# Weights times v and state times q in four column quarters of TensorE in place of two halves

## The chip, the cores and the metric

The kernel runs on one core of a Trainium2 chip. The metric is device time in microseconds (us), the median of three runs. Inputs are laid out by the host before the launch and the host does no arithmetic.

## The reference, cut to what matters

An mLSTM recurrence over 768 tokens (4 sequences, 8 heads of 40) feeds a feed-forward block of width 2048.

```python
for t in range(S):
    m_new = np.maximum(f_gate[:, :, t] + m, i_gate[:, :, t])
    f_stab = np.exp(f_gate[:, :, t] + m - m_new)
    i_stab = np.exp(i_gate[:, :, t] - m_new)
    C = f_stab * C + i_stab * einsum('bhd,bhe->bhde', vt, kt)
    n = f_stab * n + i_stab * kt
    h_tilde = einsum('bhde,bhe->bhd', C, qt)
    denom = maximum(abs(einsum('bhd,bhd->bh', n, qt)), 1.0)
    y[:, :, t] = sigmoid(o_gate) * h_tilde / denom
...
h = x @ w_in                      # x: the 3072 tokens, 320 wide
g = h * erf(softplus(h))
return g @ w_out
```

## The kernel before

The recurrence is computed in six chunks of 128 tokens. A chunk `c` of one sequence `b` is an attention step, 24 in all (`attention(s)`, with `c, b = divmod(s, 4)`). Inside a chunk the tokens meet each other through a 128x128 matrix of decay times k·q for each head (`v.w[j]`, tile `dm`); the earlier chunks come in through a state (`st`) of 82 columns for each pair of heads, kept in SBUF, which is absent in the first chunk. The feed-forward block runs in 48 groups (`mlp(g)`), each over 512 hidden columns of 256 tokens: up-projection (line 817, PSUM tile `h`), a chain of Tanh and VectorE operations, down-projection (lines 886, 887, 889, PSUM tile `po`).

Every piece of work is put into one list with a start number from tables written out by hand. The list is sorted by that number and issued in this order, so that each engine works through a fixed queue. On TensorE (PE in the profile) attention steps lie in between pieces of the feed-forward block.

The pieces of an attention step that the prediction speaks of:

- `S0`, `S1` (line 578, tile `stk`): k·q, four products with all 128 columns of the array for each half of the heads.
- `pk` (line 633): the chunk's contribution to the state, eight products whose stationary operand has 40 columns; even heads use the left half of the array's columns (output partitions 0 to 39), odd heads the right half (64 to 103). The last chunk has no `pk`, since nobody needs its state.
- `ph` (lines 614 to 624): the numerator and the denominator for 128 tokens. For each of four pairs of heads `p` it multiplies state by q (line 619, 82 moving columns, only from the second chunk on) and, for each of the two heads, the weights by v (line 623, 41 moving columns). The stationary operands are q and the weights, and their columns are tokens. The tokens are cut in two halves of 64: the output of the first half goes to PSUM partitions 0 to 63, that of the second to 64 to 127, so that the two halves use different columns of the array.
- `den` and `yg` (lines 656 and 661) read the result on ScalarE and VectorE; `tr` (line 677) transposes the normalised output on TensorE.

A product of float32 operands, as in all of these, shows in the trace as two weight loads (PEld) and two MATMULs (PE), called passes here. The feed-forward products use float32r operands and show as one.

In chunks 1 to 4 `pk` stands right before `ph` on TensorE.

Of the kernel before, what the change touches and what calls it, by code (L numbers as in the profile page):

```python
# [351 lines left out]
def tile_mlstm_moe(  # L352
# [132 lines left out]
    def psum(n, m):  # L485
        t = ps_a.tile([128, 512], F32, name="pa")
        return t[:, 0:n * m].rearrange("p (n m) -> p n m", m=m)

    def attention(s):
# [11 lines left out]
        @at('load')  # L501
        def _():
            if stacked:
                v.q = att.tile([128, NPR, L], F32, name="q_t", bufs=QB)
                v.parts = att.tile([128, 4, NPR, L], F32R, name="parts")
                v.k = v.parts.bitcast(F32)[:, 3]
                nc.sync.dma_start(v.k[0:QR], qk[c, b, :, 1])
                nc.sync.dma_start(v.q[0:QR], qk[c, b, :, 0])
            else:
                t = att.tile([128, 2, NPR, L], F32R, name="stk", bufs=SB).bitcast(F32)  # L510
                nc.sync.dma_start(t[0:QR], qk[c, b])
                v.q, v.k = t[:, 0], t[:, 1]
# [100 lines left out]
        @at('ph')  # L613
        def _():
            v.ph = psum(H, V1)
            halves = [slice(64 * i, 64 * i + 64) for i in range(2)]
            for p in range(NPR):
                for ts in halves if c > 0 else ():
                    nc.tensor.matmul(v.ph[ts, 2 * p:2 * p + 2].rearrange("p h d -> p (h d)"),  # L619
                                     v.q[0:QR, p, ts], st[0:QR, p], start=True, stop=False)  # L620
                for j in range(2):
                    for ts in halves:
                        nc.tensor.matmul(v.ph[ts, 2 * p + j], v.w[j][:, p, ts], v.v1[:, 2 * p + j],  # L623
                                         start=(c == 0), stop=(c == 0 or j == 1))
# [357 lines left out]
```

## Time and profile before

| | |
|---|---|
| median of three runs | 512.31 us (512.07 to 512.38) |
| profiled execution | 514.03 us, of which the instructions span 512.0 us |
| TensorE (PE), share of the span | 485.7 us, 95% |
| weight loads (PEld) | 455.3 us, 89% |
| VectorE (DVE) | 439.0 us, 86% |
| ScalarE (ACT) | 449.9 us, 88% |
| GpSimd (POOL) | 82.0 us, 16% |
| granted clock of TensorE, mean | 0.993 |

Times in the views are microseconds from the start of the span unless marked ns. PE are the MATMULs and PEld the weight loads, which overlap them. MATMULs are pipelined, and their ends are modelled, so that the durations of neighbours overlap: the spacing of their starts is what TensorE takes for one.

### The profile page before, as it was taken

How to read it: one execution, taken by the hardware profiler on the slowest of the kernel's cores; microseconds unless marked ns; L12 is line 12 of the kernel's file. 1: busy time of each engine (PE TensorE's matmuls, PEld its weight loads, DVE VectorE, ACT ScalarE, POOL GpSimd, SP SyncE). 2: the span in 40 equal slices, each digit the busy share in tenths (PEclk: the TensorE clock that was granted, in tenths of full speed). 3: DMA queues.
4: the chain of work that ended last, by engine and by line, in shares of the span. 5: the costliest groups of instructions: out<-in, count | busy, mean ns of one | idle time of the engine just before them, and what ended most of it. 6: DMA issues, size and time to landing. Idle time of an engine off the chain costs nothing.

```text
span 512.0 us, 11875 instructions
## 1 busy us (share of the span) xinstructions
PE 485.7 (95%) x4630; PEld 455.3 (89%) x4630; DVE 439.0 (86%) x677; ACT 449.9 (88%) x714; POOL 82.0 (16%) x112
## 2 busy tenths in 40 slices
PE   2987999899999999999999999999999999999996
PEld 1654779799899999999999999999899999999996
DVE  4868899898999999989998989989988977877653
ACT  4757899998989999889989889989889989989993
POOL 3202002211121121121121121211111211110000
PEclk9889999999999999999999999999999999999999
DMA  7995643424424415505405515415415325300000
GB/s 249 276 260 128 195 118 102 130 86 126 142 59 138 151 40 159 167 14 163 156 13 174 157 22 168 144 40 164 125 40 166 124 69 154 105 15 14 2 26 27
DMA packets 28307, 58.93 MB, mean 115 GB/s; under 512 B 4156, under 2 KB 8764, under 8 KB 28252
## 3 DMA queue, kind: packets, MB, share of 16 engines
q1 hardware_dynamic: 28252, 58.18, 38.1%
q8 instruction: 37, 0.61, 0.5%
q14 instruction: 18, 0.15, 0.1%
HBM read 33.40 MB, written 3.93 MB: 73 GB/s over the span
## 4 chain that ended last, share of the span: by engine, by line
PE 67%; ACT 11%; DVE 10%; DMA 6%; issue 4%; SPq 1%; POOL 0%; DVEq 0%; ACTq 0%
PE h L817 26%; PE po L886 9%; PE po L889 8%; PE po L887 8%; DMA stk<-parts 4%; PE pa L578 3%; PE pa L623 3%; PE pa L619 2%; PE pa L724 2%; DVE bits L712 1%; PE pa L558 1%; PE pa L633 1%; ACT n L841 1%; DMA parts<-in_qk_dram 1%; PE pa L677 1%
## 5 line engine op out<-in xcount | busy, mean ns | idle before, releaser
L817 PE MATMUL h<-xh,wh 128*128 128x256 f32 x576 | 158.9, 285 | 0.8 <-ACT hb L827 0.8
L817 PE MATMUL h<-xl,wh 128*128 128x256 f32 x576 | 156.4, 281 | 0.2 <-DVE xl L690 0.2
L886 PE MATMUL po<-woh,gh 128*128 128x320 f32 x384 | 118.2, 318 | 1.1 <-ACT gh L867 1.1
L887 PE MATMUL po<-wol,gh 128*128 128x320 f32 x384 | 114.4, 308 | 0.0
L817 PEld LDWEIGHTS h<-xh,wh 128*128 128x128 f32 x576 | 108.6, 188 | 2.6 <-ACT hb L827 1.0
L817 PEld LDWEIGHTS h<-xl,wh 128*128 128x128 f32 x576 | 108.6, 188 | 0.7 <-DVE xl L690 0.5
L817 PE MATMUL h<-xh,wl 128*128 128x256 f32 x384 | 107.7, 280 | 0.0
L889 PE MATMUL po<-woh,gl 128*128 128x320 f32 x384 | 79.2, 326 | 0.0
L569 POOL TENSOR_SCALAR_AFFINE_SELECT dm<-dm 128x512 f32<-128x512 f32 x48 | 47.0, 982 | 171.6 <-ACT dm L565 164.0
L886 PEld LDWEIGHTS po<-woh,gh 128*128 128x128 f32 x384 | 72.2, 188 | 2.3 <-ACT gh L867 1.3
L817 PEld LDWEIGHTS h<-xh,wl 128*128 128x128 f32 x384 | 72.2, 188 | 0.0
L887 PEld LDWEIGHTS po<-wol,gh 128*128 128x128 f32 x384 | 72.2, 188 | 0.0
L872 DVE TENSOR_TENSOR gl<-hb,gh 128x1024 fp32r<-128x1024 f32 x48 | 58.7, 1223 | 13.4 <-ACT gh L867 13.0
L862 DVE SCALAR_TENSOR_TENSOR hb<-n,hb 128x1024 f32<-128x1024 f32 x48 | 58.6, 1221 | 10.3 <-ACT n L858 10.1
L854 DVE SCALAR_TENSOR_TENSOR n<-n,n 128x1024 f32<-128x1024 f32 x48 | 61.6, 1284 | 4.7
L867 ACT ACTIVATE gh<-hb 128x1024 fp32r<-128x1024 f32 x48 | 50.9, 1060 | 13.2 <-DVE hb L862 10.2
L850 DVE SCALAR_TENSOR_TENSOR n<-n,hb 128x1024 f32<-128x1024 f32 x48 | 59.6, 1242 | 3.3 <-ACT n L841 3.3
L889 PEld LDWEIGHTS po<-woh,gl 128*128 128x128 f32 x384 | 61.5, 189 | 1.0
L833 ACT ACTIVATE n<-h 128x512 f32<-128x512 f32 x96 | 57.3, 597 | 1.3 <-PE h L817 1.3
L858 ACT ACTIVATE n<-n 128x1024 f32<-128x1024 f32 x48 | 51.4, 1071 | 5.9 <-DVE n L854 5.8
L827 ACT ACTIVATE hb<-h 128x512 f32<-128x512 f32 x96 | 54.6, 604 | 1.6 <-DVE gl L872 0.7
L837 ACT ACTIVATE n<-n 128x1024 f32<-128x1024 f32 x48 | 51.1, 1064 | 1.0
(102 smaller groups left out, 821.1 us busy)
## 6 DMA issues: line engine op xcount, KB each, us to landing
stk<-parts SPq DMA_DIRECT2D x120, 160.0 KB
kvo<-in_kvo_dram SPq DMA_DIRECT2D x24, 484.0 KB
parts<-in_w_out_dram SPq DMA_DIRECT2D x5, 960.0 KB
parts<-in_qk_dram SPq DMA_DIRECT2D x20, 208.0 KB
q_t<-in_qk_dram SPq DMA_DIRECT2D x20, 208.0 KB
out_dram<-o_sb SPq DMA_DIRECT2D x24, 160.0 KB
stk<-in_qk_dram SPq DMA_DIRECT2D x4, 416.0 KB
hb<-in_w_in_dram SPq DMA_DIRECT2D x2, 512.0 KB
```

The costliest lines, as they stand in the source:

```text
L817: nc.tensor.matmul(v.h[n // 2][:, n % 2 * T:(n % 2 + 1) * T], w, m, start=(q == 0), stop=(q == len(ops) - 1))
L827: nc.scalar.activation(v.hb[:, hs], v.h[i], AF.Copy)
L833: nc.scalar.activation(v.a[:, hs], v.h[i], AF.Tanh, scale=PARAMS[0], bias=PARAMS[1])
L837: nc.scalar.activation(v.a, v.a, AF.Tanh, scale=PARAMS[2], bias=PARAMS[3])
L850: nc.vector.scalar_tensor_tensor(out=v.a, in0=v.a, scalar=PARAMS[8], in1=v.hb, op0=ALU.add, op1=ALU.mult)
L854: nc.vector.scalar_tensor_tensor(out=v.a, in0=v.a, scalar=PARAMS[9], in1=v.b, op0=ALU.mult, op1=ALU.add)
L858: nc.scalar.activation(v.a, v.a, AF.Tanh, scale=PARAMS[10], bias=PARAMS[11])
L862: nc.vector.scalar_tensor_tensor(out=v.hb, in0=v.a, scalar=1.0, in1=v.hb, op0=ALU.add, op1=ALU.mult)
L872: nc.vector.tensor_tensor(v.gl, v.hb, v.gh.bitcast(F32), op=ALU.subtract)
L886: nc.tensor.matmul(po[k, b], v.gh[:, ts], woh[:, w], start=(j == 0), stop=False)
L887: nc.tensor.matmul(po[k, b], v.gh[:, ts], wol[:, w], start=False, stop=False)
L889: nc.tensor.matmul(po[k, b], v.gl[:, ts], woh[:, w], start=False, stop=(j == NFF - 1))
```

## The change

The list `halves` that cuts the 128 tokens of a step gets four slices of 32 in place of two of 64. Both inner loops of `ph` run over it, so that each product becomes two, with half the stationary columns and the same moving columns. Slice i of the output goes to PSUM partitions 32i to 32i+31.

```diff
@@ -613,7 +613,7 @@
         @at('ph')
         def _():
             v.ph = psum(H, V1)
-            halves = [slice(64 * i, 64 * i + 64) for i in range(2)]
+            halves = [slice(32 * i, 32 * i + 32) for i in range(4)]
             for p in range(NPR):
                 for ts in halves if c > 0 else ():
                     nc.tensor.matmul(v.ph[ts, 2 * p:2 * p + 2].rearrange("p h d -> p (h d)"),
```

On TensorE's queue in a step of the second chunk, from the last up-projection before `ph` to its first pair of heads; the numbers behind a name are output partitions x moving columns, and x4 stands for four in a row. Before:

```order
L817 MATMUL h<-xl,wh 128x256
L578 MATMUL pa<-stk 128x128 x4
L633 MATMUL pa<-vg,kvo 40x41 x8
L619 MATMUL pa<-state_85,q_t 64x82 x2
L623 MATMUL pa<-kvo,dm 64x41 x4
```

And with the change:

```order
L817 MATMUL h<-xl,wh 128x256
L578 MATMUL pa<-stk 128x128 x4
L633 MATMUL pa<-vg,kvo 40x41 x8
L619 MATMUL pa<-state_85,q_t 32x82 x4
L623 MATMUL pa<-kvo,dm 32x41 x8
```

The pieces keep their places; for a pair of heads line 619 issues four products in place of two, line 623 eight in place of four.

On TensorE's queue in a step of the first chunk, as a difference (line 581 is k·q there, lines 724 and 725 unpack the weights of the feed-forward block):

```order
 L725 MATMUL pa<-woh,nident 128x320
 L581 MATMUL pa<-stk 128x128 x4
-L623 MATMUL pa<-kvo,dm 64x41 x16
+L623 MATMUL pa<-kvo,dm 32x41 x32
 L724 MATMUL pa<-bits,ident 128x320
 L725 MATMUL pa<-woh,nident 128x320
```

Here too nothing changes its place. The first chunk has no product with the state.

## Rows read from the trace of the kernel before

**Rows 1.** The page, parts 1 and 2: the span, busy time, granted clock in 40 slices.

```profile
span 512.0 us, 11875 instructions
PE 485.7 (95%) x4630; PEld 455.3 (89%) x4630; DVE 439.0 (86%) x677; ACT 449.9 (88%) x714; POOL 82.0 (16%) x112
PEclk9889999999999999999999999999999999999999
```

**Rows 2.** Busy time by stretch: PE, PEld, DVE, ACT, POOL, clock, DMA.

```profile
0.00:60.00 60.00, 44.02 (x290) 29.57 (x291) 43.84 (x96) 38.94 (x85) 11.19 (x30) 0.94 0.80 231
...
257.76:295.16 37.40, 37.40 (x396) 36.43 (x392) 34.92 (x56) 33.93 (x53) 6.25 (x8) 1.00 0.38 116
```

**Rows 3.** Chain that ended last, by line; then pieces of it: start, us, what.

```profile
by line: PE h L817 26.0%; PE po L886 9.0%; PE po L889 8.3%; PE po L887 8.1%; DMA stk<-parts 4.2%; issue 3.6%; PE pa L578 2.9%; PE pa L623 2.8%; PE pa L619 2.3%; PE pa L724 2.0%; DVE bits L712 1.5%; PE pa L558 1.3%; PE pa L633 1.3%; ACT n L8
...
220.53 0.16 PE pa L619 x4
220.70 0.21 PE pa L623 x8
...
354.87 6.84 DMA stk<-parts
```

**Rows 4.** PE in order of time around one `ph`: start, us, engine, line, operation, count.

```profile
220.03 0.51 PE L633 MATMUL pa<-vg,kvo 128*40 128x41 f32 x16
220.37 0.33 PE L619 MATMUL pa<-state,q_t 104*64 104x82 f32 x4
...
220.74 0.34 PE L619 MATMUL pa<-state,q_t 104*64 104x82 f32 x4
...
221.66 0.38 PE L623 MATMUL pa<-kvo,dm 128*64 128x41 f32 x8
221.97 0.41 PE L886 MATMUL po<-woh,gh 128*128 128x320 f32 x1
222.22 0.31 PE L887 MATMUL po<-wol,gh 128*128 128x320 f32 x1
222.37 0.31 PE L886 MATMUL po<-woh,gh 128*128 128x320 f32 x1
```

**Rows 5.** PEld in order of time in the same `ph`.

```profile
220.71 0.20 PEld L619 LDWEIGHTS pa<-state,q_t 104*64 104x64 f32 x4
220.84 0.33 PEld L623 LDWEIGHTS pa<-kvo,dm 128*64 128x64 f32 x8
221.08 0.20 PEld L619 LDWEIGHTS pa<-state,q_t 104*64 104x64 f32 x4
```

**Rows 6.** PE instructions of line 619 begun by the end of each stretch (in brackets).

```profile
220.36:220.37 0.01, 0.00 (x1) 1.00 0.00 0
220.36:220.38 0.01, 0.01 (x2) 1.00 0.00 0
```

**Rows 7.** Groups by line and shape: busy us, mean ns of one.

```profile
L623 PE MATMUL pa<-kvo,dm 128*64 128x41 f32 x768 | 34.8, 222 | 0.0
...
L677 PE MATMUL pa<-ident,kvo 128*128 128x128 f32 x72 | 12.1, 274 | 0.2 <-POOL kvo L671 0.2
L633 PE MATMUL pa<-vg,kvo 128*40 128x41 f32 x320 | 10.4, 209 | 0.0
...
L623 PEld LDWEIGHTS pa<-kvo,dm 128*64 128x64 f32 x768 | 30.7, 138 | 1.0 <-PE pa L724 0.5 <-issue 0.3
...
L633 PEld LDWEIGHTS pa<-vg,kvo 128*40 128x40 f32 x320 | 8.0, 120 | 2.9 <-PE pa L677 1.0 <-DVE bits L711 0.6 <-issue 0.4
```

**Rows 8.** PE in order of time where the last chunk's `ph` follows a transpose.

```profile
417.68 0.49 PE L677 MATMUL pa<-ident,kvo 128*128 128x128 f32 x3
418.10 0.36 PE L619 MATMUL pa<-state,q_t 104*64 104x82 f32 x4
```

**Rows 9.** PE in order of time, a `ph` of the first chunk.

```profile
35.73 1.13 PE L623 MATMUL pa<-kvo,dm 128*64 128x41 f32 x32
```

## The prediction

> **What bounds the kernel now.** I read the page first [rows 1]. PE is busy for 95% of the span, and its clock is granted in full (2.4 GHz, the higher of its two levels) from the second slice on. The profiled execution took 514.03 us, 1.7 us above the median of 512.31 us; I make the sum against it and carry the difference over.
>
> A busy share averages over stages, so I read the stretches next [rows 2]. In the first 60 us PE is busy for 44.0 us and waits for weights that are being unpacked. From 257.76 to 295.16 us, as in the other steady stretches, it is busy for all of 37.40 us, while DVE and ACT have 2.5 and 3.5 us to spare. There, time taken from PE is time taken from the kernel, as long as it is less than about 2 us in 37.
>
> The third view is the chain of waits [rows 3]. Line 619 has 2.3% of it and line 623 has 2.8%, of 512 us: 11.8 and 14.3 us. One `ph` puts four pieces of each on it, 0.16 and 0.21 us long, 0.64 and 0.84 us together. So some 17 or 18 executions of `ph` with the state lie on the chain. There are 20 of these (chunks 1 to 5), and the four of the first chunk, which have line 623 alone, find no place in the 14.3 us. I count 17, of which 13 come right behind `pk` and 4 are the last chunk's.
>
> **What one `ph` is made of.** In time order [rows 4] a group (one pair of heads: 4 passes of line 619, 8 of line 623) takes 220.74 - 220.37 = 0.37 us, four take 1.5 us. Passes start in twos: the first of line 619 by 220.37, the second by 220.38 us [rows 6], one in each half of the columns. I call such a pair a round; a group has 2 rounds of line 619 and 4 of line 623. The weight loads show where the time goes [rows 5]: from 220.71 to 220.84 for line 619, 0.13 us or 65 ns a round, and from 220.84 to 221.08 for line 623, 0.24 us or 60 ns a round. Line 623 streams 41 columns, half of line 619's 82, and still takes nearly as long. So streaming does not set its round; loading 64 columns of weights does. The neighbour `pk` confirms it: it streams the same 41 columns against 40 columns of weights, and its 8 rounds take 220.37 - 220.03 = 0.34 us, 42 ns each [rows 4]. One of its loads lasts 120 ns against 138 ns [rows 7], 0.75 ns for a column.
>
> **The change, part by part.** The passes of a `ph` go from 48 to 96 (from 32 to 64 in the first chunk), each with half the columns of weights. What counts is how many run side by side. If four quarters run abreast as two halves do now, a group still has 2 + 4 rounds, and only the length of a round changes.
>
> *Rounds of line 623.* Now 60 ns. With 32 columns of weights, at most the 42 ns of `pk` with 40; at least half of line 619's 65 ns, 33 ns, because 41 columns have to be streamed. I take 40 ns, close to the nearest row. Gain: 4 rounds x 20 ns x 4 groups = 0.32 us a `ph`, bounds 0.29 and 0.43.
>
> *Rounds of line 619.* They last 65 ns with loads that would allow 60, so streaming sets them and a shorter load gives nothing: 0.
>
> *Two more starts in each round.* Now the second start follows within 10 ns [rows 6]. The third and fourth could fall inside the round (0) or lengthen it by 10 ns each: 20 ns x 24 rounds = 0.48 us a `ph`. I take 0, since the second start today lies inside a round that its own load or stream fills, and keep 0.48 for the range.
>
> *The width changes between `pk` and `ph`.* Both use halves now: the last pass of `pk` begins at 220.03 + 0.51 - 0.20 = 220.34 us, and line 619 0.03 us later [rows 4]. Where the width changes, the trace shows a gap. The last transpose before the last chunk's `ph`, a full-width product, begins at 417.68 + 0.49 - 0.27 = 417.90 us, and line 619 at 418.10, 0.20 us later [rows 7, 8]. Behind a `ph`, the last pass begins at 221.66 + 0.38 - 0.22 = 221.82 us, the next product 0.15 us later, and that one takes 0.25 us where its neighbour takes 0.15 [rows 4, 7]. With the change `pk` stays in halves and `ph` goes to quarters. No row shows such a change: between 0 (as if it were none) and 0.23 us more (0.15 + 0.10 as at the exit, less a load of 32 columns). I take 0.15, the 0.20 of rows 8 less today's 0.03 and less 0.02 for the shorter load, since every change of width in the trace costs about that. It falls on the 13 executions behind `pk`.
>
> The Trainium skill (TensorEngine Tiling (Array Packing), section Tiling Modes) lists 64 and 32 columns as separate configurations and says that a change of configuration drains the engine while a change of tile does not. By that rule the 0.15 us is paid; without it the sum below would be -5.5 us. The trace agrees for full width against halves (0.20 and 0.03 us), and no run here shows halves against quarters yet.
>
> *The two other borders.* Entry from full width (the last chunk) gains the shorter load, 0.02 us; the exit to full width waits for the last pass as now: 0.
>
> *The first chunk.* Its four `ph` take 1.13 us each [rows 9] and would shorten by 16 rounds x 20 ns = 0.32 us, but none lies on the chain; nor do three of the later ones. I count 0 and keep 4 x 0.32 + 3 x 0.17 = 1.8 us as a bound on the gain.
>
> *Other engines.* DVE, ACT, POOL and the queues of DMA issues get the same work in the same order. Their cover in the steady stretches is 2.5 us in 37; a period holds two `ph`, which take some 0.35 to 0.7 us from it.
>
> **Sum.** 13 x (0.32 - 0.15) + 4 x (0.32 + 0.02) = 2.2 + 1.4 = 3.6 us gained; I say 3.5. The profiled execution would take 510.5 us, the median 508.8 us.
>
> **Rivals.**
>
> *Slower: PE is not fed twice as fast.* Doubling the passes pays only if they start at more than the rate of now. The fastest that the trace shows is `pk`, 16 passes in 0.34 us, 21 ns each; a `ph` in quarters wants 96 in about 1.2 us, 12 ns each. If 21 ns is the rate at which passes can be fed, a `ph` takes 96 x 21 ns = 2.0 us in place of 1.5: 0.5 us lost, 0.65 with the change of width; 13 x 0.65 + 4 x 0.5 = 10.5 us, a median of 523. It decides from 15.6 ns a pass (1.5 us / 96), without the width change. Against it: the two passes of a round of `pk` or line 619 start within 10 ns of each other and then nothing starts until the load or the stream is done, so 21 ns is a round divided by two and need not be a limit. Chance 0.13.
>
> The Trainium skill has a rule that speaks for this rival (TensorEngine Tiling (Array Packing), section Instruction Overhead): each matmul carries some 60 cycles of overhead, and a dimension that is already small should not be tiled for. By an estimate from that figure, 60 cycles at 2.4 GHz or 25 ns a pass in sequence, a `ph` would take 2.4 us and the kernel some 17 us more. Rows 6 do not bear it out as a cost in sequence, with two starts within 10 ns.
>
> *Slower: only two quarters run abreast.* Then a group has 4 rounds of 65 ns and 8 of 40 ns, 0.58 us against 0.37: 0.84 us a `ph`, with the width change 13 x 0.99 + 4 x 0.84 = 16 us, a median of 528. It would be so if PE looks ahead over few passes: a quarter's next work stands behind two passes of each of the three others, a half's behind two of one. No row shows how far it looks. Chance 0.07.
>
> *No change.* The starts lengthen the rounds by half of their bound (0.24 us a `ph`) and the width change costs its 0.23; or PE comes earlier and waits for something else, as it does at 354.87 us, where a DMA of 6.84 us lies on the chain [rows 3]. Then 512 us. Chance 0.14. That the edit does not do what it says has little room: the queue shows 32 partitions and twice the products in each place. I leave it in these 0.14.
>
> *The forecast* has the remaining 0.66.
>
> **Range and chances.** The forecast's own bounds: at best 13 x 0.43 + 4 x 0.45 + 1.8 = 9.2 us gained (503.1 us), with all borders free and all of the early gains kept; at worst, with the starts in sequence and the dear border, a loss of 13 x 0.4 + 4 x 0.15 = 5.8 us (518.1 us). Both ends need every unknown to fall on one side. The range from 504.5 to 513.0 us holds most of the forecast and the case of no change, and leaves out the two slower rivals, 0.2 together. A measurement of this kernel tells about 0.2% (1.0 us) from nothing. Faster by more: 0.66; within: 0.14; slower: 0.20.
>
> **What would show it.** In the profile after: weight loads of line 623 with 32 columns, near 114 ns (138 - 32 x 0.75); four passes of line 619 begun within some 20 ns; a group in about 0.29 us in place of 0.37; line 619 some 0.18 us behind the last pass of `pk`; stretches of 37.4 us shorter by 0.3 to 0.4 us, with PE still busy throughout. A group of 0.5 us or more, with passes spaced evenly at about 21 ns, makes the first rival right; a group near 0.58 us with starts in twos the second. A shorter `ph` with the same period would mean that PE was not the bound there, and my count of 17 on the chain was wrong.

## The result, and the profile after

The changed kernel takes 507.79 us in the median of ten runs (505.95 to 511.54), the kernel before 512.2 us (510.68 to 513.66) in runs on the same chip: a ratio of 0.9916 with a 95% interval of 0.9891 to 0.9941, 4.4 us less. The forecast was 508.8 us, in a range of 504.5 to 513.0.

The page of the changed kernel, parts 1 to 3 (span and busy time; the queue that brings instructions):

```profile
span 504.1 us, 14051 instructions
PE 478.0 (95%) x5718; PEld 447.5 (89%) x5718; DVE 438.5 (87%) x677; ACT 447.7 (89%) x714; POOL 82.2 (16%) x112
...
q8 instruction: 45, 0.74, 0.6%
```

There are 1088 more MATMULs and as many more weight loads than before [rows 1], and PE is busy for 7.7 us less. The spans of these two traces differ by 7.9 us, more than the change is worth: 1.6 us of it had passed before the first `ph` began (28.82 us here, 30.43 us before), a piece of the program that the change does not touch, and 1.7 us are waits of line 578 for the DMA of `stk` (4.1 us in the first trace of before, 2.4 here). The first of the two goes with the clock: ahead of the first `ph` TensorE was granted its lower level (1.2 GHz, 0.50 in the view) for 6.83 us before and for 3.41 us here. The same columns as in [rows 2], before and after:

```profile
21.75:28.58 6.83, 6.76 (x31) 4.54 (x32) 4.72 (x11) 4.13 (x10) 0.00 (x0) 0.50 1.04 264
```

```profile
23.90:27.31 3.41, 3.41 (x22) 2.01 (x18) 2.68 (x6) 2.23 (x5) 0.00 (x0) 0.50 1.04 333
```

The experiments take the rest apart.

Busy time by stretch, the period that answers to the second line of [rows 2] and the next one (PE, PEld, DVE, ACT, POOL, clock, DMA):

```profile
254.18:291.21 37.03, 37.03 (x487) 35.98 (x483) 34.95 (x56) 33.72 (x53) 6.18 (x8) 1.00 0.39 117
291.21:328.23 37.02, 37.02 (x487) 35.97 (x483) 35.05 (x54) 34.80 (x54) 7.80 (x9) 1.00 0.37 115
```

A period of two steps lasts 37.03 us in place of 37.40, and PE still has no gap in it; DVE and ACT do the work of before in less time.

One `ph` on PE in time order, as in [rows 4] (start, us, engine, line, operation, count), then three lines of its weight loads, as in [rows 5]:

```profile
253.80 0.45 PE L633 MATMUL pa<-vg,kvo 128*40 128x41 f32 x14
254.18 0.35 PE L619 MATMUL pa<-state,q_t 104*32 104x82 f32 x8
254.35 0.33 PE L623 MATMUL pa<-kvo,dm 128*32 128x41 f32 x16
254.50 0.33 PE L619 MATMUL pa<-state,q_t 104*32 104x82 f32 x8
254.64 0.33 PE L623 MATMUL pa<-kvo,dm 128*32 128x41 f32 x16
254.79 0.33 PE L619 MATMUL pa<-state,q_t 104*32 104x82 f32 x8
...
255.23 0.33 PE L623 MATMUL pa<-kvo,dm 128*32 128x41 f32 x16
255.50 0.42 PE L886 MATMUL po<-woh,gh 128*128 128x320 f32 x1
255.75 0.31 PE L887 MATMUL po<-wol,gh 128*128 128x320 f32 x1
```

```profile
254.47 0.17 PEld L619 LDWEIGHTS pa<-state,q_t 104*32 104x32 f32 x8
254.57 0.28 PEld L623 LDWEIGHTS pa<-kvo,dm 128*32 128x32 f32 x16
254.76 0.17 PEld L619 LDWEIGHTS pa<-state,q_t 104*32 104x32 f32 x8
```

A group lasts 254.79 - 254.50 = 0.29 us with 24 passes, where it lasted 0.37 us with 12. By the starts of the MATMULs line 619 holds 0.14 us of it (254.50 to 254.64, 72 ns a round) and line 623 0.15 us (38 ns a round). The prediction read its rounds from the starts of the weight loads, which divide a group otherwise, so each has to be compared with its like. By the loads, the two rounds of line 619 in a group went from 131 to 110 ns and the four of line 623 from 246 to 185 ns; by the MATMULs, from 172 to 144 and from 205 to 151 ns (medians over the later groups of all 20 `ph` with state). Both ways line 619 gives a part of what is saved.

The other ends of the `ph` moved too. The last pass of `pk` begins at 253.80 + 0.45 - 0.21 = 254.04 us and line 619 0.14 us later (0.130 us by the single starts), where it was 0.03. The last pass of line 623 begins at 255.23 + 0.33 - 0.20 = 255.36 us and the next full-width product 0.14 us later, where it was 0.15 (0.128 and 0.160 us by the single starts).

Groups by line and shape: mean duration in ns behind the busy time. A load of 32 columns lasts 110 ns (138 before; the prediction said 114).

```profile
L623 PEld LDWEIGHTS pa<-kvo,dm 128*32 128x32 f32 x1536 | 24.9, 110 | 1.0 <-PE pa L724 0.4 <-issue 0.3
```

MATMULs of line 619 begun by the end of each stretch, as in [rows 6]:

```profile
254.17:254.19 0.02, 0.01 (x2) 1.00 0.00 0
254.17:254.20 0.03, 0.02 (x3) 1.00 0.66 273
254.17:254.21 0.04, 0.03 (x4) 1.00 0.50 205
```

Four passes, one in each quarter, begin within 0.03 us, at most 10 ns apart; by the single starts of this row the next begins 95 ns behind the first. Quarters run abreast.

### The profile page after: what moved, and what is told of

It reads as the page before. It is cut to its first block, busy times and chain, and to the rows that moved or that the text cites. A ratio compares the mean times of both kernels' runs of the same rounds, so it can differ in the third digit from the quotient of the medians.

```text
span 504.1 us, 14051 instructions
## 1 busy us (share of the span) xinstructions
PE 478.0 (95%) x5718; PEld 447.5 (89%) x5718; DVE 438.5 (87%) x677; ACT 447.7 (89%) x714; POOL 82.2 (16%) x112
## 4 chain that ended last, share of the span: by engine, by line
PE 72%; ACT 12%; DVE 10%; issue 3%; DMA 2%; SPq 0%; POOL 0%; DVEq 0%; ACTq 0%
PE h L817 29%; PE po L886 10%; PE po L889 9%; PE po L887 9%; PE pa L578 3%; PE pa L619 3%; PE pa L623 2%; DVE bits L712 2%; PE pa L558 1%; PE pa L633 1%; DMA stk<-parts 1%; PE pa L677 1%; ACT gh L867 1%; DVE bits L711 1%; ACT bits L706 1%
```

## The experiments

### The change and the kernel before, a second trace of each

The change, with no edit:

> The changed kernel once more, for a second trace and a closer time. Theory (quarters run abreast, what is saved is saved at the executions of ph on the chain): each ph behind pk 0.19 us shorter (1.447 + 0.029 + 0.160 us became 1.185 + 0.130 + 0.129 in the first trace), each of the last chunk 0.32 us, together 13 x 0.19 + 4 x 0.32 = 3.8 us, or 5.6 us if all 24 count; ratio to before 0.989 to 0.993. Rival (the 7.9 us between the two spans is what the change is worth): ratio 0.985.

The kernel before, with no edit:

> The kernel before once more, for a second trace. Theory (the waits for DMA near 210 and 360 us, 0.9 and 1.2 us, and the slower first 30 us of its first trace are not the change's): they come and go from run to run, here too. Rival (the change removes them): both waits are here again, at the same places, and in neither trace of the changed kernel.

Measured: the change 508.18 us, ratio 0.9934 (0.9911 to 0.9958); the kernel before 510.76 us in one run. Of the waits for the DMA of `stk` on PE the page of before, again, and of the change, again, show (line waited for: us in total, times, longest us):

```profile
PE pa L578 <- DMA stk<-parts: 2.5, 3, 1.5
```

```profile
PE pa L578 <- DMA stk<-parts: 2.6, 4, 1.5
```

So these waits vary from run to run between 2.4 and 4.1 us, and 2.5 us was there without the change: the rival of both expectations falls. The first `ph` began at 30.43 and 29.07 us before, at 28.82 and 31.82 us after; that, too, is no effect of the change but goes with the clock. In the second trace of before no lower level is on record between 16.20 us and its first `ph`. In that of the change the clock of this time is not on record, but MATMULs of line 724 still last 0.74 us at 25.8 us, as they do in all four traces at 12.6 us, where the kernel before, again, has 0.43 us from 17.1 us on.

What is the change's can be read between fixed points inside one trace. First the kernel before, again, then the change, then the change, again: the first `ph` with state and the last one.

```profile
106.58 0.34 PE L619 MATMUL pa<-state,q_t 104*64 104x82 f32 x4
...
451.89 0.36 PE L619 MATMUL pa<-state,q_t 104*64 104x82 f32 x4
```

```profile
106.50 0.33 PE L619 MATMUL pa<-state,q_t 104*32 104x82 f32 x5
...
447.54 0.35 PE L619 MATMUL pa<-state,q_t 104*32 104x82 f32 x8
```

```profile
109.47 0.35 PE L619 MATMUL pa<-state,q_t 104*32 104x82 f32 x8
...
451.24 0.35 PE L619 MATMUL pa<-state,q_t 104*32 104x82 f32 x8
```

345.31 us before, 341.04 and 341.77 us after: 3.5 to 4.3 us. In these stretches PE waited for 2.1, 1.6 and 2.1 us. The first trace of before has 346.79 us (108.25 to 455.04) with 2.9 us of waits. Less the waits, the stretch takes 343.2 and 343.9 us before and 339.4 and 339.7 us after, 4.0 us less in the mean. From the starts of single passes, a `ph` behind `pk` is 0.19 us shorter from border to border, and one of the last chunk 0.32 us. Of 20, 16 stand behind `pk`; 19 lie between the two points: 16 x 0.19 + 3 x 0.32 = 4.0 us, too.

### Every `ph` with state computed twice, in halves and in quarters

```diff
-            for p in range(NPR):
+            for p in list(range(NPR)) * (2 if c > 0 else 1):
```

In quarters:

> Every ph with state computed twice in a row into the same place (the first product of the second round starts the sum anew): 96 more passes in each of 20 steps, 4 groups of 0.295 us, 1.18 us. Theory (17 of 20 lie on the chain and the steady stretches are bound by PE): 17 x 1.18 = 20 us above the changed kernel, 528; all 20: 531.5. Rival (PE has slack in these stretches, the gain came from elsewhere): under 10 us. If the feeding of passes fell behind in long rows, the second four groups would take more than 0.295 us each.

In halves:

> The kernel before, in halves, with every ph with state computed twice in a row: 48 more passes in each of 20 steps, 4 groups of 0.376 us, 1.50 us. Theory (the waits of 1 to 3 us in the changed kernel's doubled rows come from the loading of instructions, 16 KB at a time: quarters use them up at twice the rate, 16 passes and their loads in a group's 0.295 us against 8 in 0.376): no wait in these rows, 20 x 1.50 = 30 us above the kernel before, 542; 17 of 20: 537. Rival (repeating a ph is itself what waits): rows with waits of 1 to 3 us as in quarters, 555 or more.

Measured: in halves 541.47 us against 511.21, 30.3 us more (ratio 1.0593, 1.0567 to 1.062). Each `ph` is 1.50 us longer, and 30.3 / 1.50 = 20.2 (19 to 21 by the interval): all 20 count here, and my 17 from the chain of waits was too few.

In quarters 563.05 us, 55 us above the change (ratio to before 1.1002, 1.0969 to 1.1034): neither theory nor rival of that expectation, but its last sentence. The first groups take their 0.29 us, then in 8 of the 20 rows PE stands still, with over 0.25 us between two starts. PE in time order in one of them (in brackets the idle time and what ended it):

```profile
250.59 0.33 PE L619 MATMUL pa<-state,q_t 104*32 104x82 f32 x8
250.74 0.25 PE L623 MATMUL pa<-kvo,dm 128*32 128x41 f32 x4
253.94 0.31 PE L623 MATMUL pa<-kvo,dm 128*32 128x41 f32 x11 [2.96 <-issue]
```

"issue" is idle time in which PE waited for nothing that the profile shows. Its waits of this kind by line (us in total, times, longest):

```profile
PE pa L623 <- issue: 10.7, 6, 3.0
...
PE po L887 <- issue: 3.3, 1, 3.3
...
PE pa L619 <- issue: 2.9, 2, 1.5
PE po L886 <- issue: 2.8, 1, 2.8
```

No such wait of PE is among those of the kernel before, of the change, or of the doubled halves. What they wait for is shown by the DMA queue that brings instructions. On the pages it moved 37 packets before, 45 after the change and 60 here, each of 16,384 bytes in the DMA records: 15 packets for the 3840 instructions that the doubling adds, 256 instructions each. The waits in the eight rows ended 1.2 to 1.6 us after such a packet had landed; the one above at 253.94, with a packet landing at 252.54 us. DMA queues of that kernel from 251.6 to 252.6 us (packets, MB, share of 16 engines):

```profile
q8 instruction: 1, 0.02, 5.6%
```

So PE had used up the instructions in store and waited for the next 256. A doubled row in quarters is 384 instructions in 2.4 us, in halves 192 in 3.0 us; the halves never waited, so that the repetition itself is not the cause. That a packet's landing ended the waits is a matter of times that agree in all eight; the store itself is not in the trace. Of the 55 us, 20 x 1.18 = 23.6 are the passes and 19.7 the waits in the lines above. A good part of the other 12 us is the clock, which fell to its lower level four times behind the longest waits; two of these stretches, with the columns of [rows 2] (the clock is the 0.50):

```profile
255.25:258.66 3.41, 3.41 (x15) 3.21 (x14) 2.76 (x8) 1.61 (x4) 0.24 (x1) 0.50 0.00 0
384.95:388.36 3.41, 3.41 (x19) 3.41 (x14) 2.73 (x6) 1.73 (x3) 0.23 (x1) 0.50 0.02 5
```

The first begins 1.3 us behind the wait shown above, the second 0.6 us behind one of 2.65 us; the other two begin at 210.87 and 340.58 us, behind the waits of 2.8 and 3.3 us. In them products of lines 886 and 887 start every 0.27 us in place of 0.15, so that the 13.7 us at the lower level cost about 6 us, an estimate from these two spacings. Another 3.1 us had passed before the first `ph` (31.91 us against 28.82 in the first trace of the change; 31.82 in its second). The profiled execution is the shortest of the four, 561.17 us; the other three had a mean granted clock of 0.975 to 0.979, against its 0.988.

### Six groups in place of four

```diff
-            for p in range(NPR):
+            for p in (0, 1, 2, 3, 0, 1) if c > 0 else range(NPR):
```

> The changed kernel with six groups in each ph with state in place of four (the first two computed again): 1.77 us in place of 1.18, 0.59 us more in each of 20 steps. In the rows of eight groups the first wait came 1.68 us behind the first pass at the earliest. Theory (instructions in store last for about that long): no wait or a few short ones in the rows, 20 x 0.59 = 12 us above the changed kernel, 520. Rival (each pass beyond the change's own number waits): as much per pass as in the doubled rows, 55 us / 2 = 27 us, 535.

Measured: 523.71 us, ratio 1.0253 (1.0221 to 1.0285): 15.7 us above the change (508 us), nearer to the 12 of the theory than to the 27. Most rows take their 1.77 us; in three more than 0.25 us lies between two starts. The longest, in time order:

```profile
349.52 0.32 PE L623 MATMUL pa<-kvo,dm 128*32 128x41 f32 x12
351.35 0.27 PE L623 MATMUL pa<-kvo,dm 128*32 128x41 f32 x4 [1.50 <-issue]
```

The last pass before it began 1.8 us behind the row's first (347.88 us). The row of the change ends after 1.19 us, short of this.

### The products of the first chunk four times

```diff
-                for j in range(2):
+                for j in [0, 1] * (4 if c == 0 else 1):
```

> The changed kernel with each product of the first chunk's four ph issued four times (each writes the same result): 16 rounds of 37 ns become 64, 1.8 us more in each of four steps, 7.1 us in all. Theory (none of the four lies on the chain): within 1.5 us of the changed kernel. Rival (they count as the others do, and the change gained some 1.2 us there): 7 us slower, 515.

Measured: 523.27 us, ratio 1.0213 (1.0181 to 1.0245), 15 us above the change. It did not answer its question, since here, too, PE ran out of instructions: its rows are four times as long, and the waits for "issue" are 11.3 us.

```profile
PE pa L623 <- issue: 9.9, 5, 3.7
...
PE po L887 <- issue: 1.4, 1, 1.4
```

Behind the first of them (2.36 us, ended at 32.42 us) the clock fell as well, to its lower level for 10.24 us:

```profile
32.69:42.93 10.24, 6.56 (x149) 4.17 (x135) 1.75 (x4) 2.28 (x6) 0.00 (x0) 0.50 0.30 113
```

With waits, clock and 7.1 us of passes in the same stretch, what the passes alone would have cost can't be told from this run. For the size of the change the next experiment tells more.

### Two quarters at a time

```diff
-            for p in range(NPR):
-                for ts in halves if c > 0 else ():
+            for two in (halves[0:2], halves[2:4]):
+                for p in range(NPR):
+                    for ts in two if c > 0 else ():
...
-                    for ts in halves:
+                        for ts in two:
```

> The same 96 passes of a ph in another order: first all groups for the tokens of quarters 0 and 1, then all for quarters 2 and 3, so that two quarters run abreast. Theory (the gain comes from four abreast; a round is the longer of load and stream, whatever the number of quarters in it): the rounds double, 0.58 us for what is a group now, 1.15 us more a ph; 17 of them 20 us, 528. Rival (what counts is the number of passes and the length of their loads, not how many run abreast): 507.5.

Measured: 528.53 us, ratio 1.0328 (1.0283 to 1.0372), 20.5 us above the change, as the theory had it, though by two misses that cancel: by its starts a `ph` got 1.05 us longer and not 1.15, and 20 of them make 21 us, where 17 would make 18. PE in time order (line numbers are one higher here):

```profile
309.84 0.32 PE L624 MATMUL pa<-kvo,dm 128*32 128x41 f32 x8
309.99 0.31 PE L620 MATMUL pa<-state,q_t 104*32 104x82 f32 x4
310.13 0.32 PE L624 MATMUL pa<-kvo,dm 128*32 128x41 f32 x8
310.29 0.31 PE L620 MATMUL pa<-state,q_t 104*32 104x82 f32 x4
```

A group of 12 passes takes 0.30 us, as the change's group of 24 does: the length of a round does not depend on whether it holds two quarters or four, and the gain is that four of them fit in it.

The same trace settles the first chunk for small amounts. Its four `ph` have 64 passes each as in the change, but last 0.47 us longer each (1.09 us from the first pass to the last against 0.62). From the first `ph` (31.93 us) to the first with state (109.59 us) it takes 77.66 us, the change 28.82 to 106.50, 77.68 us. 1.9 us more on PE moved nothing.

### Widths mixed within a `ph`

```diff
+            wide = [slice(64 * i, 64 * i + 64) for i in range(2)]
             for p in range(NPR):
-                for ts in halves if c > 0 else ():
+                for ts in wide if c > 0 else ():
```

> State times q in halves as before the change, weights times v in quarters: the width changes 7 times inside each ph with state. Theory (each change of width costs 0.10 to 0.15 us): pk to ph gains 0.10 back, 7 changes lose 0.7 to 1.0 us; 0.6 to 0.9 us a ph, 17 of them 10 to 15 us above the changed kernel, 518 to 523. Rival (changes between halves and quarters are free and only the shorter loads count): 506 to 508.

Measured: 524.12 us, ratio 1.0238 (1.0207 to 1.0268), 16 us above the change, a little over the theory's upper end. By the starts a `ph` behind `pk` is 0.88 us longer from border to border than in the change and one of the last chunk 1.01 us: all 20 would be 18.1 us, 17 (13 and 4) 15.5. PE in time order:

```profile
301.47 0.34 PE L620 MATMUL pa<-state,q_t 104*64 104x82 f32 x4
301.74 0.36 PE L624 MATMUL pa<-kvo,dm 128*32 128x41 f32 x16
302.03 0.36 PE L620 MATMUL pa<-state,q_t 104*64 104x82 f32 x4
```

A group takes 0.58 us (302.03 + 0.58 = 302.61 for the next) where it takes 0.29 without the two changes of width in it: 0.14 us each, or 0.13 if line 619 in halves is counted with the 0.17 us that it took before. `pk` runs straight into line 620 again, since both are halves.

### `pk` in quarters too

```diff
-                        nc.tensor.matmul(v.pk[64 * j:64 * j + D, p], v.kn[:, 2 * p + j], v.vg[j][:, p], start=True, stop=True)
+                        for lo, hi in ((0, 32), (32, D)):
+                            nc.tensor.matmul(v.pk[64 * j + lo:64 * j + hi, p], v.kn[:, 2 * p + j, lo:hi], v.vg[j][:, p],
+                                             start=True, stop=True)
```

> pk too in quarters: the 40 columns of a head as 32 and 8, on output partitions 64j to 64j+31 and 64j+32 to 64j+39. Theory (the change from halves to quarters costs 0.10 us each time, and a round is the longer of load and stream): line 619 follows the last pass of pk by 0.03 us as before the change, the 8 rounds of pk take 38 ns in place of 42; 0.13 us less in each of 16 steps, 1.7 us (13 on the chain) to 2.1 us below the changed kernel, 506. Rival (the 0.10 us is the latency of the last passes of pk, whatever their width): the gap stays at 0.13 us and the time at 507.5. Rival (passes are fed at no more than 21 ns each): the 32 passes of pk take 0.67 us in place of 0.34, 4 us slower.

> pk and ph in quarters once more, for a closer time. In its first trace the gap between pk and line 619 is 0.01 us in place of 0.13 us, and undisturbed periods of two steps last 36.77 us against 37.02. Theory: 16 x 0.12 = 2 us below the changed kernel, 506 where that takes 508; ratio to before 0.988 to 0.990. Rival (what PE saves there comes back as waits for the DMA of stk): the ratio of the change, 0.992 to 0.993.

Measured: 507.1 us, ratio 0.9903 (0.9879 to 0.9927), and the second time 506.39 us, 0.99 (0.9873 to 0.9927). In time order `pk` (line 634 here) and `ph`:

```profile
255.18 0.50 PE L634 MATMUL pa<-vg,kvo 128*32 128x41 f32 x32
255.49 0.34 PE L619 MATMUL pa<-state,q_t 104*32 104x82 f32 x8
255.64 0.35 PE L623 MATMUL pa<-kvo,dm 128*32 128x41 f32 x16
```

`pk` takes 0.31 us with 32 passes in place of 0.34 with 16, and the gap to line 619 is gone: the 0.10 us of the change was the change of width. Both times this version was 1.1 to 1.8 us below the change in the median, where the trace gives 16 x 0.12 = 2 us, but the intervals overlap with the change's; it is faster than the kernel before in both, but that it is faster than the change is shown by the traces of `pk` and `ph` and not by the times. The row of `pk` and `ph` is now 256 instructions long, and in the second trace one of the 16 such rows waited for them:

```profile
144.06 0.31 PE L619 MATMUL pa<-state,q_t 104*32 104x82 f32 x3
144.72 0.27 PE L619 MATMUL pa<-state,q_t 104*32 104x82 f32 x3 [0.34 <-issue]
```

## Why the prediction was right, and where it was off

*The clock in full from the second slice on.* Misread: the second and third slice have an 8 in [rows 1], which is the stretch of 6.83 us at the lower level shown above. It lies ahead of the first `ph`, so no term of the sum hangs on it, but it may be a part of why that execution was longer than the median.

*Two passes for each product.* This holds for `pk` and `ph`. Line 578 (160 MATMULs for 160 products) and line 677 (72 for 72) show one pass each; the sum does not count them.

*PE bounds the steady stretches.* Right: the periods lost 0.37 us and PE stayed busy; no other engine took over.

*Seventeen executions on the chain.* Too few. The doubled halves cost 20.2 times their own length, two quarters at a time 20.5 / 1.05 = 19.5 times; only the mixed widths, with 16 us, lie nearer to 17 than to 20. The chain of waits follows one path; executions that it went round were paid as well. The time of the change itself can't tell: 17 give 13 x 0.19 + 4 x 0.32 = 3.8 us, 20 give 4.3, and 4.4 and 3.4 us were measured, each with an interval of more than 1 us to either side.

*The first chunk counts for nothing.* Right for amounts such as the change's: 1.9 us more there did not move the first `ph` with state, and the change's 1.2 us less did not either: from the first `ph` to the first with state it took 77.8 and 77.5 us before, 77.7 us in both traces after.

*Rounds of line 623, 60 to 40 ns, and of line 619, unchanged.* The split was wrong and the total right, by luck. Read from the loads as the prediction did, a round of line 623 went from 62 to 46 ns and one of line 619 from 66 to 55; by the MATMULs it was 51 to 38 and 86 to 72. So line 623 gave 54 to 61 ns a group where 80 was forecast, and line 619, put at 0 because streaming would set its rounds, gave 21 to 28. The two errors cancel: a group lost 0.08 us, 0.32 a `ph`, as the sum had it. Why a shorter load helps line 619, too, no run here takes apart. The first group of a `ph` behind `pk` gives back 0.03.

*Two more starts.* At most 10 ns each, inside the round, as I took it.

*The width change, 0.15 us.* It is 0.10 at this border and 0.13 to 0.14 inside a `ph`. The 0.20 us of [rows 8] from which the 0.15 came held the last transpose's own time: the three transposes start at 417.68, 417.79 and 417.90 us, 0.11 us apart, so that the change of width after them cost 0.09 us, close to what was then measured. By the Trainium skill (TensorEngine Tiling (Array Packing), section Tiling Modes) changing the tiling mode drains the engine; the pauses in the mixed widths and their absence with `pk` in quarters agree, while the draining itself is not in the trace.

*The sum.* 16 x 0.19 + 4 x 0.32 = 4.3 us in place of 13 x 0.17 + 4 x 0.34 = 3.6; measured 4.4, and 3.4 in the second set of runs. By the traces the forecast of 3.5 us was some 0.8 us short because of the count and the width change; the two measured times lie on either side of it.

*The rivals.* Passes fed no faster than 21 ns: not in a `ph` of the change, 96 passes in 1.19 us, 12 ns each. The rule of the Trainium skill on which it leaned (same page, section Instruction Overhead, some 60 cycles a matmul) does not hold as a cost in sequence with four column tiles. But the point behind this rival, that PE has to be fed, is real: not as a rate for each pass but as a store that runs empty in longer rows. Only two quarters abreast: excluded by the starts in fours and by the order that forces it.

## What to carry to other kernels

Where small products have moving operands so short that weight loads set their pace, cutting the stationary side into quarters that run abreast pays by what the shorter load takes off a round (13 of 51 ns and 14 of 86 ns here, by the MATMULs), and each change of column width beside it costs 0.10 to 0.14 us; keep neighbours at one width. In a stretch where PE has no gaps, count every execution and not just those on the chain of waits. Where a gap between two starts is to tell the price of a change of width, take off what the product before the gap lasts by itself. And count instructions: here rows of up to 224 in 1.5 us ran through, of 32 rows of 256 one waited, rows of 320 and of 416 did more often, for up to microseconds at a time, and behind the longest waits, in the rows of 416, the clock fell.

## What the runs showed of the hardware that I had not expected

PE can run out of instructions. They come in packets of 16,384 bytes, 256 instructions by the count of packets; in and right behind rows of short passes PE stood idle for up to 3.3 us, and each of the eight such waits inside rows ended 1.2 to 1.6 us after a packet had landed. In the doubled rows none began earlier than 1.7 us behind the first pass. Four times the granted clock then fell from 2.4 to 1.2 GHz for 3.4 us, each time within 1.6 us of the end of a wait of 2.7 to 3.3 us, so that running out of instructions was paid for twice.
